# Agent attention with two dense layers on one core: everything up to the sixteenth tile pair written as single-engine steps

## The chip, the cores and the metric

One core of a Trainium2 chip runs the whole program. The metric is the device time of one execution in microseconds (us). Five engines work side by side, each through its own queue in order: TensorE (PE) multiplies matrices, VectorE (DVE), ScalarE (ACT) and GpSimd (POOL) work on elements, and SyncE (SP) issues the transfers. They wait for each other only through semaphores.

## The reference

```python
s = scale * (agents @ k.T); a2k = softmax(s)        # 49 agents over 12480 keys
agent_v = a2k @ v                                   # 49 x 128
x = softmax(scale * (q @ agents.T)) @ agent_v       # 12480 x 128
h = x @ moe_w_in                                    # 128 -> 2048
x = where(h > 0, h, exp(min(h, 0)) - 1) @ moe_w_out # 2048 -> 128
h = x @ moe2_w_in
out = (max(h, 0) + alpha * min(h, 0)) @ moe2_w_out
```

All inputs are float32 except the four weight matrices, which arrive as 64-bit words (float64) and are turned into float32 on the chip.

## The kernel before

The first stretch is the agents' attention over k and v. Both come in ten pieces of 1280 rows (the last of 960, cut into eight chunks of 120). `S0` to `S9` are the score matmuls of a piece: each chunk of 128 keys is the stationary operand and meets `agd`, the agents written twice (98 columns, line 491); the scores go to two PSUM banks and are copied to the tile `S` (501), while VectorE keeps the running maximum `top` (504). The pieces form two halves of five, each with its own maximum: `D` turns the column maxima with a matmul (513), 514 and 515 reduce and spread them, `X` brings them back across (519). `E` subtracts the maximum (524), takes exp (528) and adds up (531, 533). `A` multiplies with v (562). `N` computes the shares of the two halves (543 to 553). Then `normalize` (592 to 594) makes `avn`, the agents' values, and `fold` (603 to 614) multiplies them into the first layer's weights, four slices `s1`, so that layer one becomes one matmul on the query probabilities.

Queries go through in 25 blocks (384, six of 480, eighteen of 512). Their softmax is the chain `q_split` to `q_place`: scores, a 32 by 32 transpose, maximum, exp, sums, weighing, transpose back, and five small transfers that place the result (276, 277).

The layers run in 200 tile pairs u, eight a block, each two chunks of 128 hidden columns. `g1` makes h (630, 633), `g1_act` and `g1_elu` the ELU (640, 641, 648 or 652 and 654), `g2` the product with the second matrix (676, or three matmuls through `mm3`, 431 to 433, once weights and activations are split in a high and a low part), `g3` and `g4` the second layer. `slot(s)` issues two pairs of layer one together with pairs ten behind of layer two.

There are sixteen weight slices w0 to w15, four each of the four matrices. `decode` turns a slice from 64-bit words into float32: two ScalarE reads (`da` 339, `dr` 340), two VectorE bit operations (352, 355), an addition on GpSimd (361, 366), and for the second layer a scaling (370), a rounded copy (372) and a rest (373). `linear` multiplies the alpha part of layer two into one 128 by 128 matrix (390 to 405).

What sets the order: loads follow the table `LOADS`, from a ring of nine buffers for k and v and four for weights. The first stretch follows `ORDER`, in which `T2` advances the decoding and `Q2` the first query chain. In the first stretch and in slots 0 to 10 only SyncE's queue keeps the written order; the other engines' queues are filled by the scheduler from its own estimate of when things are ready. `normalize` and the first two folds between them, and everything from slot 12 on, keep the written order on all queues.

Of the kernel before, what the change touches and what calls it, by code (L numbers as in the profile page):

```python
# [8 lines left out]
F32 = mybir.dt.float32  # L9
# [14 lines left out]
PIECES = [(i * 1280, 10, 128) for i in range(9)] + [(11520, 8, 120)]  # L24
# [33 lines left out]
def agent_attention_moe_kernel(  # L58
# [33 lines left out]
    hps = ctx.enter_context(tc.tile_pool(name="hps", bufs=3, space=bass.MemoryType.PSUM))  # L92
# [20 lines left out]
    agd = const.tile([P, 2, A], F32, name="agd")  # L113
# [69 lines left out]
    def q_max(b):  # L183
        n = blocks[b][1]
        st = q_st[b]
        j = n // 32
        m, m2 = qsmall("m"), qsmall("m2")
        nc.vector.tensor_reduce(out=m[:, :j], in_=by32(st, n), axis=AX.X, op=ALU.max)
        (nc.scalar.copy if b < Q_FIRST else nc.vector.tensor_copy)(out=m2[:32, :j], in_=m[32:, :j])
        q_st[b] = st, m, m2  # L190

    def q_less(b):
        n = blocks[b][1]
        st, m, m2 = q_st[b]
# [47 lines left out]
    def q_norm_4(b):  # L242
# [3 lines left out]
        nc.vector.reciprocal(out=r[:32, :j], in_=s2[:32, :j])  # L246
        (nc.scalar.copy if b < Q_FIRST else nc.vector.tensor_copy)(out=r[32:, :j], in_=r[:32, :j])
        q_st[b] = e, r

    def q_weigh(b):  # L250
# [4 lines left out]
        nc.gpsimd.tensor_tensor(  # L255
# [16 lines left out]
    def q_place(b):  # L272
# [8 lines left out]
        -3: [q_split], 3: [q_scores], 4: [q_sum, q_add], 6: [q_turn], 8: [q_max], 9: [q_less], 11: [q_exp],  # L281
        12: [q_norm_1], 14: [q_norm_2], 15: [q_norm_3], 16: [q_norm_4], 17: [q_weigh], 18: [q_turn], 19: [q_hi],
# [7 lines left out]
    free = {"kv": KV, "w": RAW}  # L290
# [3 lines left out]
    def pump():  # L294
        while todo:
# [7 lines left out]
            if kind == "k":  # L303
                t0, nch, m = PIECES[i]
                kt[i] = rings["kv"].tile([P, 10, P], F32, tag="kv", name="kt").rearrange("p c d -> p (c d)")
                cut = [0, 512, nch * m] if i == 0 else [0, nch * m]
                for lo, hi in zip(cut, cut[1:]):
                    nc.sync.dma_start(out=kt[i][:, lo:hi], in_=kT[:, t0 + lo:t0 + hi])
            elif kind == "v":
                t0, nch, m = PIECES[i]  # L310
                vt[i] = rings["kv"].tile([P, 10, P], F32, tag="kv", name="vt")
                src = vm[:, i * 1280:(i + 1) * 1280] if m == P else vl
                nc.sync.dma_start(out=vt[i][:m, :nch, :].rearrange("p c d -> p (c d)"), in_=src)
# [16 lines left out]
    ahead = []  # L330
    flying = []
    started = [0]

    def decode(i):
        name, j = SLICES[i]
        src = words.pop(i)
        x = dec.tile([P, 4, P], F32, tag="da", name="da")
        r = dec.tile([P, 4, P], U32, tag="dr", name="dr")
        nc.scalar.activation(out=x, in_=src[:, :, :, 1].bitcast(F32), func=AF.Copy, scale=2.0 ** -112)
        nc.scalar.activation(out=r, in_=src[:, :, :, 0], func=AF.Copy, scale=2.0 ** -29)  # L340
        free["w"] += 1
        pump()
        yield
        sl = slice(4 * j, 4 * j + 4)
        if name == "wo1":
            w = wo1w[j] = wo.tile([P, 4, P], F32, tag="wo1", bufs=9, name="wo1w")
            g = w.bitcast(U32)
        else:
            g = w1[j].bitcast(U32) if name in ("wi1", "wo2") else dec.tile([P, 4, P], U32, tag="dg", bufs=2, name="dg")
        t = spare().rearrange("p (f c) -> p f c", c=P).bitcast(U32)  # L350
        xu = x.bitcast(U32)
        nc.vector.tensor_scalar(
            out=t, in0=xu, scalar1=4, scalar2=1, op0=ALU.logical_shift_left, op1=ALU.logical_shift_right
        )
        nc.vector.scalar_tensor_tensor(
            out=g, in0=xu, scalar=0x80000000, in1=t, op0=ALU.bitwise_and, op1=ALU.bitwise_or
        )
        if name in ("wi1", "wo1"):
            done.add(i)
            yield  # L360
            nc.gpsimd.tensor_tensor(out=g, in0=g, in1=r, op=ALU.add)
            return
        h, l = {"wi2": (wi2h, wi2l), "wo2": (wo2h, wo2l)}[name]
        h, l = h[:, sl, :], l[:, sl, :]
        gf = g.bitcast(F32)
        nc.gpsimd.tensor_tensor(out=g, in0=g, in1=r, op=ALU.add)
        yield
        if name == "wo2":
            v = dec.tile([P, 4, P], U32, tag="dg", bufs=2, name="dx").bitcast(F32)
            nc.vector.tensor_tensor(out=v, in0=gf, in1=oma[:, sl].unsqueeze(2).to_broadcast([P, 4, P]), op=ALU.mult)  # L370
            gf = v
        nc.scalar.copy(out=h, in_=gf)
        (nc.vector if i in REST_DVE else nc.gpsimd).tensor_tensor(out=l, in0=gf, in1=h.bitcast(F32), op=ALU.subtract)
        done.add(i)

    def split(j):
        w = wo1w.pop(j)
        h = wo1h[j] = wo.tile([P, 4, P], F32R, tag="wo1", bufs=9, name="wo1h")
# [4 lines left out]
    def linear():

        for j in range(4):
            sl = slice(4 * j, 4 * j + 4)
            t4 = hpair()[:, 0, :].rearrange("p (f c) -> p f c", c=P)
            for f in range(4):
                for x in (wi2h, wi2l):
                    nc.tensor.matmul(t4[:, f, :], x[:, 4 * j + f, :], unit, start=x is wi2h, stop=x is wi2l)  # L390
            kt_ = dec.tile([P, 4, P], F32, tag="da", name="da")
            nc.vector.tensor_tensor(
                out=kt_, in0=t4, in1=al[:, sl].unsqueeze(2).to_broadcast([P, 4, P]), op=ALU.mult
            )
            yield
            tw = hpair()[:, 0, :P]
            for f in range(4):
                nc.tensor.matmul(tw, kt_[:, f, :], w1[j][:, f, :], start=f == 0, stop=f == 3)
            if j == 0:
                nc.vector.tensor_copy(out=lin, in_=tw)  # L400
            else:
                nc.vector.tensor_tensor(out=lin, in0=lin, in1=tw, op=ALU.add)
            yield
        nc.scalar.copy(out=linh, in_=lin)
        nc.vector.tensor_tensor(out=linl, in0=lin, in1=linh.bitcast(F32), op=ALU.subtract)
        done.add("lin")

    lines = linear()
    folded = set()

    def spare():

        return hpair()[:, 0, :] if 0 in o_ps or 0 in y_t or not ahead else bank("o", 1)

    def micro(n):

        while n > 0:
            ran = False
            for x in list(flying):
                if next(x, "end") == "end":  # L420
                    flying.remove(x)
                ran = True
                n -= 1
            if len(flying) < 2 and started[0] in words and (SLICES[started[0]][0] != "wo2" or len(folded) == 4):
                flying.append(decode(started[0]))
                started[0] += 1
            elif not ran:
                return
# [422 lines left out]
```

## Time and profile before

| | |
|---|---|
| three runs, median (lowest to highest) | 1082.84 us (1082.27 to 1084.37) |
| the profiled execution | 1083.18 us |
| its span in the trace | 1081.40 us |
| busy: PE, DVE, ACT, POOL | 97%, 77%, 75%, 57% of the span |

Outside the span lie 1.78 us, of which the trace shows nothing. A busy PE may still be slow: its clock is granted at 1.2 or 2.4 GHz, and its short matmuls are not all at the rate of the array. Shares over the whole span hide that the first tenth looks different from the rest, so the views below cut it in stages.

### The profile page before, as it was taken

To read this page: it belongs to the slowest core of one execution; us is meant where nothing else is said; L and a number is where in the kernel's file an instruction comes from. 1 tells how busy PE (TensorE), PEld (TensorE's weight loads), DVE (VectorE), ACT (ScalarE), POOL (GpSimd) and SP (SyncE) were. 2 spreads that over 40 slices of the span, in tenths; PEclk is the share of its full clock that TensorE was granted. 3 is DMA by queue.
4 is the path that set the end of the run, shared out by engine and by line. 5 is a ranking of instruction groups with operands and counts; after the bars stand their busy time and mean duration, and the time that the engine had idled before them with its cause. 6 is when DMAs were issued, how large, how long until landed. Compare 5 with 4: busy or idle time off the path is not lost.

```text
span 1081.4 us, 13413 instructions
## 1 busy us (share of the span) xinstructions
PE 1053.1 (97%) x5029; PEld 831.9 (77%) x5029; DVE 830.9 (77%) x932; ACT 811.1 (75%) x944; POOL 613.4 (57%) x349
## 2 busy tenths in 40 slices
PE   7788999999999999999999999999999999999998
PEld 6635888888888777777777777777777777777776
DVE  5866687878878788788788788788787787787653
ACT  5587677777777877877877877777777777777763
POOL 3656655665555665565565565565565566555440
PEclk9888999999999999999999999999999999999999
DMA  9920000000010010010010010000000000000000
GB/s 357 375 89 19 20 8 28 19 19 20 20 29 10 20 30 10 20 30 10 21 30 10 21 30 13 26 22 15 25 20 19 22 20 20 20 10 20 11 1 20
DMA packets 17915, 41.34 MB, mean 38 GB/s; under 512 B 3345, under 2 KB 6303, under 8 KB 17851
## 3 DMA queue, kind: packets, MB, share of 16 engines
q1 hardware_dynamic: 17707, 40.36, 11.5%
q8 instruction: 40, 0.66, 0.3%
q14 instruction: 24, 0.20, 0.1%
q10 hardware_dynamic: 144, 0.13, 0.0%
HBM read 27.60 MB, written 6.39 MB: 31 GB/s over the span
## 4 chain that ended last, share of the span: by engine, by line
PE 91%; DVE 3%; ACT 2%; DMA 2%; issue 1%; POOL 1%; SPq 0%; DVEq 0%; POOLq 0%; ACTq 0%
PE o L431 10%; PE o L433 9%; PE o L432 9%; PE h L630 8%; PE h L433 8%; PE h L431 8%; PE h L432 8%; PE y L431 8%; PE y L432 8%; PE y L433 8%; PE h L633 4%; DMA kt<-in_kT_dram 1%; DMA wi<-in_w_in_dram 1%; PE h L159 1%; ACT e L640 0%
## 5 line engine op out<-in xcount | busy, mean ns | idle before, releaser
L665 POOL TENSOR_TENSOR gl<-g,gh 128x1024 fp32r<-128x1024 f32 (+1 forms) x192 | 454.0, 2370 | 258.4 <-DVE gh L654 170.7
L706 DVE SCALAR_TENSOR_TENSOR xl<-h,xh 128x1024 fp32r<-128x1024 f32 (+3 forms) x201 | 239.7, 1192 | 127.4 <-ACT xh L705 125.8
L705 ACT ACTIVATE xh<-h 128x1024 fp32r<-128x1024 f32 (+3 forms) x201 | 201.3, 1002 | 177.3 <-PE h L433 175.9
L652 DVE SCALAR_TENSOR_TENSOR g<-e,h 128x1024 f32<-128x1024 f32 (+1 forms) x192 | 229.0, 1193 | 71.6 <-ACT e L641 55.5
L640 ACT ACTIVATE e<-h 128x1024 f32<-128x1024 f32 (+2 forms) x200 | 199.2, 996 | 30.2 <-PE h L633 26.4
L641 ACT ACTIVATE e<-e 128x1024 f32<-128x1024 f32 (+2 forms) x200 | 207.9, 1040 | 6.1
L431 PE MATMUL o<-xh,wo2h 128*128 128x512 f32 (+2 forms) x400 | 162.1, 405 | 2.8 <-ACT xh L705 2.8
L433 PE MATMUL o<-xh,wo2l 128*128 128x512 f32 (+2 forms) x400 | 154.5, 386 | 0.0
L433 PE MATMUL h<-yh,wi2l 128*128 128x512 f32 (+2 forms) x400 | 154.4, 386 | 0.0
L431 PE MATMUL h<-yh,wi2h 128*128 128x512 f32 (+2 forms) x400 | 154.4, 386 | 0.0
L432 PE MATMUL o<-xl,wo2h 128*128 128x512 f32 (+2 forms) x400 | 154.3, 386 | 0.0
L432 PE MATMUL h<-yl,wi2h 128*128 128x512 f32 (+2 forms) x400 | 154.1, 385 | 0.0
L431 PE MATMUL y<-gh,wo1h 128*128 128x512 f32 (+1 forms) x384 | 149.1, 388 | 0.0
L432 PE MATMUL y<-gl,wo1h 128*128 128x512 f32 (+1 forms) x384 | 148.4, 386 | 0.0
L433 PE MATMUL y<-gh,wo1l 128*128 128x512 f32 (+1 forms) x384 | 148.3, 386 | 0.0
L654 DVE SCALAR_TENSOR_TENSOR gh<-e,h 128x1024 fp32r<-128x1024 f32 (+1 forms) x96 | 115.0, 1198 | 0.0
L630 PE MATMUL h<-pst,s 128*128 128x512 f32 (+2 forms) x400 | 110.6, 396 | 3.2 <-DVE gh L648 1.0
L431 PEld LDWEIGHTS o<-xh,wo2h 128*128 128x128 f32 x400 | 75.1, 188 | 32.1 <-ACT xh L705 14.7
L663 ACT CAST gh<-g 128x1024 fp32r<-128x1024 f32 (+1 forms) x96 | 98.7, 1028 | 1.1 <-DVE g L652 1.1
L630 PEld LDWEIGHTS h<-pst,s 128*128 128x128 f32 x400 | 75.0, 190 | 22.3 <-issue 1.9
L431 PEld LDWEIGHTS h<-yh,wi2h 128*128 128x128 f32 x400 | 75.4, 188 | 14.7 <-issue 0.2
L433 PEld LDWEIGHTS o<-xh,wo2l 128*128 128x128 f32 x400 | 75.3, 188 | 14.6
(149 smaller groups left out, 1302.9 us busy)
## 6 DMA issues: line engine op xcount, KB each, us to landing
vt<-in_vm_dram SPq DMA_DIRECT2D x9, 640.0 KB
kt<-in_kT_dram SPq DMA_DIRECT2D x8, 640.0 KB
q<-in_qT_dram SPq DMA_DIRECT2D x18, 256.0 KB
psq<-pst SPq DMA_DIRECT2D x72, 64.0 KB
out_dram<-o SPq DMA_DIRECT2D x17, 256.0 KB
wi<-in_w_in_dram SPq DMA_DIRECT2D x8, 512.0 KB
wo<-in_w_out_dram SPq DMA_DIRECT2D x8, 512.0 KB
q<-in_qT_dram SPq DMA_DIRECT2D x6, 240.0 KB
```

What stands on the lines that cost most here:

```text
L431: nc.tensor.matmul(out, w_hi, x_hi, start=start, stop=False)
L432: nc.tensor.matmul(out, w_hi, x_lo, start=False, stop=False)
L433: nc.tensor.matmul(out, w_lo, x_hi, start=False, stop=stop)
L630: nc.tensor.matmul(h_t[u + v][:, c, :], s1[:, i + 2 * v + c, :], pst[b][:, :n], start=True, stop=False)
L640: nc.scalar.activation(out=e, in_=h_t[u], func=AF.Relu, scale=-1.0)
L641: nc.scalar.activation(out=e, in_=e, func=AF.Exp, scale=-1.0)
L652: nc.vector.scalar_tensor_tensor(out=g, in0=e, scalar=-1.0, in1=h, op0=ALU.add, op1=ALU.max)
L654: nc.vector.scalar_tensor_tensor(out=gh, in0=e, scalar=-1.0, in1=h, op0=ALU.add, op1=ALU.max)
L663: nc.scalar.copy(out=gh, in_=g)
L665: nc.gpsimd.tensor_tensor(out=gl, in0=g, in1=gh.bitcast(F32), op=ALU.subtract)
L705: nc.scalar.activation(out=xh[:, c, :], in_=h[:, c, :], func=AF.Relu)
L706: nc.vector.scalar_tensor_tensor(out=xl[:, c, :], in0=h[:, c, :], scalar=0.0, in1=xh[:, c, :].bitcast(F32), op0=ALU.max, op1=ALU.subtract)
```

## The change

`ORDER` becomes a list of about 530 steps, one for one engine each, from the first score matmul to the last step ahead of slot 16; every engine's queue keeps that order from the start, and `slot` begins at 16. Decoding falls into eight steps (`x r t o a v h l`), the ELU of a pair into `e`, `E`, `g.`, `gc`, `gl`, the query chain into its single instructions. A list `OTHER` puts some of them on another engine than usual. The piece of k and v at the end is cut into 128-row chunks and one of 64 rows. A score chunk becomes two matmuls of 64 keys by 49 agents in two column halves, and a piece's scores fit one PSUM bank, six of which go round. The maxima `mc` and the shares are kept in PSUM, and the shares are applied to the values instead of to the turning matrix. `LOADS` brings k and v ahead of most weights.

```diff
 LOADS = """
-    w0 k0 w1 k1 q0 w2 k2 w3 k3 w4 k4 k5 w5 k6 k7 k8 k9 w6 v0 v1 w7 v2 v3 v4 w8 v5 v6 w9 v7 v8 w10 v9 a0 q1
-    w11 w12 w13 w14 w15
+    k0 q0 k1 k2 k3 k4 k5 k6 k7 w0 z0 w1 k8 k9 v0 v1 v2 v3 v4 v5 q1 v6 w2 v7 v8 w3 v9 w4 w5 w6 w7 w8 w9 w10 a0 w11
+    w12 q2 q3 w13 w14 w15
 """
 ORDER = """
-    T2 S0 T2 S1 Q2 T2 S2 Q2 S3 T2 Q2 S4 D0 Q2 T2 S5 X0 E0 Q2 S6 T2 E1 Q2 S7 E2 T2 S8 Q2 E3 T2 Q2 S9 D1 E4 A0 X1 A1 T2
...
+    S0 q0.qh q0.ql C0 q0.sc S1 q0.sl q0.sa q0.t1 S2 C1 M1 q0.mx S3 M2 C2 q0.m2 q0.ms q0.mc M3 S4 C3 q0.d q0.ex C4 S5
...
+OTHER = """
+    C0 C4 C5 K1 K7 e11 e13 e15 e2 e6 e8 l9 q0.wg v11 v13 v15 v9
+""".split()
+FIRST = 16
...
         def scores(i):
-            sp = hpair()
-            for c in range(nch):
-                o = sp[:m, c // 5, 2 * A * (c % 5):2 * A * (c % 5) + 2 * A]
-                nc.tensor.matmul(o, kt[i][:, c * m:(c + 1) * m], ag, start=True, stop=True)
+            sp[i] = single()[:, :10 * A].rearrange("p (c a) -> p c a", a=A)
+            for c in range(nch):
+                for p0 in (0, AP):
+                    col = c * m + p0 * (PIECES[i][0] + c * m + p0 < NTOK)
+                    nc.tensor.matmul(sp[i][p0:p0 + AP, c, :], kt[i][:, col:col + AP], ag, start=True, stop=True)
...
-            nc.vector.tensor_tensor(out=mc[:, 2:3], in0=mc[:, 0:1], in1=mc[:, 1:2], op=ALU.max)
-            nc.vector.tensor_scalar(out=cs, in0=mc[:, 0:2], scalar1=mc[:, 2:3], scalar2=None, op0=ALU.subtract)
+        mc = across[:, AP + 4:AP + 6]
+                nc.vector.tensor_reduce(out=rs[:, 4:5], in_=mc, axis=AX.X, op=ALU.max)
+                nc.vector.tensor_tensor(out=cs, in0=mc, in1=rs[:, 4:5].to_broadcast([P, 2]), op=ALU.subtract)
...
+    def negative(u):
+        e = e_t[u] = wide("e", F32, of(u)[2])
+        if f"e{u}" in OTHER:
+            nc.vector.tensor_scalar(out=e, in0=h_t[u], scalar1=0.0, scalar2=None, op0=ALU.min)
+        else:
+            nc.scalar.activation(out=e, in_=h_t[u], func=AF.Relu, scale=-1.0)
```

The first place is SyncE's queue at the start. Its rows before (`kt` is a piece of k, `wi` and `wo` a weight slice, `agp` the agents):

```order
L440 DMA agp<-in_agT_dram 128x64
L317 DMA wi_149<-in_w_in_dram 128x1024
L308 DMA kt<-in_kT_dram 128x512
L308 DMA kt<-in_kT_dram 128x768
L317 DMA wi_154<-in_w_in_dram 128x1024
L308 DMA kt<-in_kT_dram 128x1280
```

and now:

```order
L510 DMA agp<-in_agT_dram 128x64
L348 DMA kt<-in_kT_dram 128x512
L348 DMA kt<-in_kT_dram 128x768
L150 DMA q<-in_qT_dram 128x384
L348 DMA kt<-in_kT_dram 128x1280 x7
L358 DMA wi_168<-in_w_in_dram 128x1024
```

The first weight slice moved from ahead of the first piece of k to behind the eighth; further on, eleven weight slices stood ahead of the last piece of v, and four do now.

The second place is VectorE from the second maximum on. Before (`pm<-top` and `su<-acc` close a half's maximum and sum, `h<-da` and the row with `da,h` decode):

```order
L506 TENSOR_REDUCE pm<-top 128x49
L352 TENSOR_SCALAR h<-da 128x512
L514 TENSOR_REDUCE mc<-o 128x1
L524 TENSOR_TENSOR S<-S,o 128x490
L355 SCALAR_TENSOR_TENSOR wo1w<-da,h 128x512
L515 COPY mb<-mc 49x128
L543 TENSOR_TENSOR mc<-mc 128x1
L544 TENSOR_SCALAR cs<-mc 128x2
L524 TENSOR_TENSOR S<-S,o 128x490 x4
```

and now, where `o` is the PSUM bank that holds the maxima:

```order
L579 TENSOR_REDUCE pm<-top 128x49
L405 SCALAR_TENSOR_TENSOR w_1_95<-da,hb 128x512
L592 TENSOR_REDUCE o<-o 128x1
L593 COPY mb<-o 49x128
L665 TENSOR_REDUCE rs<-o 128x1
L666 TENSOR_TENSOR cs<-o,rs 128x2
L603 TENSOR_TENSOR S<-S,o 128x490 x2
L603 TENSOR_TENSOR S<-S,o 128x392
L603 TENSOR_TENSOR S<-S,o 128x490 x2
```

The small steps read PSUM instead of the tile `mc`, and one decoding row stands here instead of two.

The third place is VectorE behind the last row of the first stretch, the copy to `avn` (`s` and `s1q` are a fold's results, `gh` the ELU of a pair). Before:

```order
L593 COPY avn<-o 128x128
L352 TENSOR_SCALAR o<-da 128x512
L355 SCALAR_TENSOR_TENSOR w_0_97<-da,o 128x512
L352 TENSOR_SCALAR o<-da 128x512
L611 SCALAR_TENSOR_TENSOR s_84<-hi,low,h 128x512
L614 TENSOR_TENSOR s1q<-h,hi 128x128
```

and now:

```order
L685 COPY avn<-o 128x128
L391 TENSOR_SCALAR o<-da 128x512
L405 SCALAR_TENSOR_TENSOR wo1w<-da,o 128x512
L391 TENSOR_SCALAR o<-da 128x512
L405 SCALAR_TENSOR_TENSOR wo1w<-da,o 128x512
L716 SCALAR_TENSOR_TENSOR s_81<-hi,low,h 128x512
L719 TENSOR_TENSOR s1q<-h,hi 128x128
```

Two slices are decoded between the copy and the first fold's result, and they are the first ones of `moe_w_out` (`wo1w`), which before were decoded ahead of the copy.

## Rows read from the trace of the kernel before

**Rows 1.** The page: granted TensorE clock in 40 slices, tenths of full speed.

```profile
PEclk9888999999999999999999999999999999999999
```

**Rows 2.** Stages: length, busy us (count) by engine, clock, DMA share, GB/s.

```profile
0.00:59.13 59.13, 42.58 (x419) 39.18 (x419) 37.93 (x72) 33.25 (x68) 30.59 (x43) 0.94 0.95 348
59.13:103.30 44.17, 36.35 (x133) 18.07 (x134) 32.00 (x51) 35.67 (x62) 25.87 (x24) 0.84 0.14 47
103.30:143.78 40.48, 40.23 (x228) 35.11 (x227) 29.02 (x41) 27.11 (x34) 24.76 (x14) 0.96 0.05 13
143.78:1081.40 937.62, 933.94 (x4254) 739.51 (x4252) 731.97 (x769) 715.08 (x783) 532.22 (x269) 1.00 0.07 19
```

**Rows 3.** TensorE in order of time: start, us, line, operands, count [idle before].

```profile
13.71 2.44 PE L491 MATMUL h<-agd,kt 128*128 128x98 f32 x20
...
24.27 0.44 PE L513 MATMUL o<-ident,pm 128*64 128x128 f32 x4 [0.17 <-DVE pm L506]
...
30.59 4.12 PE L491 MATMUL h<-agd,kt 128*128 128x98 f32 x36 [0.72 <-ACT S L501]
34.64 2.39 PE L562 MATMUL y<-vt,S 128*49 128x128 f32 x40
...
58.20 0.54 PE L592 MATMUL o<-by,avs 128*128 128x160 f32 x2 [0.69 <-DVE avs L571]
59.13 1.12 PE L603 MATMUL h<-w,avn 128*128 128x512 f32 x2 [0.39 <-DVE avn L593]
...
72.26 2.93 PE L676 MATMUL y<-gh,wo1w 128*128 128x384 f32 x4
```

**Rows 4.** Stages of the loading, columns as in rows 2.

```profile
0.00:20.00 20.00, 12.74 (x87) 12.24 (x88) 9.07 (x22) 11.76 (x25) 7.74 (x22) 1.00 0.90 339
20.00:40.00 20.00, 17.68 (x183) 16.45 (x182) 17.67 (x31) 12.85 (x25) 13.24 (x14) 1.00 1.02 410
40.00:50.00 10.00, 5.48 (x68) 5.08 (x70) 7.87 (x12) 4.49 (x10) 6.35 (x7) 0.75 1.03 374
```

**Rows 5.** SyncE, then ScalarE, in order of time.

```profile
40.08 0.41 SPq L313 DMA_DIRECT2D vt<-in_vl_dram  x1
...
5.55 0.66 ACT L339 ACTIVATE da<-wi 128x512 f32<-128x512 f32 x1 [2.23 <-DMA wi<-in_w_in_dram]
```

**Rows 6.** VectorE, groups by form: count, busy us, mean ns, idle before.

```profile
L352 DVE TENSOR_SCALAR h<-da 128x512 uint32<-128x512 uint32 x11 | 7.5, 686 | 5.0 <-ACT da L339 4.8
L648 DVE SCALAR_TENSOR_TENSOR gh<-e,h 128x768 f32<-128x768 f32 x8 | 7.5, 936 | 5.3 <-ACT e L641 5.2
L506 DVE TENSOR_REDUCE pm<-top 128x49 f32<-128x490 f32 x2 | 2.0, 1011 | 0.1
```

**Rows 7.** VectorE in order of time, around the second maximum.

```profile
39.19 1.01 DVE L515 COPY mb<-mc 49x128 f32<-49x128 f32 x1
40.13 1.23 DVE L543 TENSOR_TENSOR mc<-mc 128x1 f32<-128x1 f32 x1
41.40 1.16 DVE L544 TENSOR_SCALAR cs<-mc 128x2 f32<-128x2 f32 x1
42.47 2.85 DVE L524 TENSOR_TENSOR S<-S,o 128x490 f32<-128x490 f32 x5
...
53.54 0.16 DVE L546 TENSOR_TENSOR rs<-o,cs 128x2 f32<-128x2 f32 x1 [0.38 <-PE o L542]
```

**Rows 8.** GpSimd in order of time, the same stretch.

```profile
40.07 1.27 POOL L361 TENSOR_TENSOR wo1w<-wo1w,dr 128x512 uint32<-128x512 uint32 x1
41.30 1.23 POOL L531 TENSOR_TENSOR acc<-S,acc 128x490 f32<-128x490 f32 x1
```

**Rows 9.** ScalarE and GpSimd, groups by form.

```profile
L340 ACT ACTIVATE dr<-wo 128x512 uint32<-128x512 uint32 x8 | 5.4, 670 | 0.3 <-POOL wo1w L361 0.3
L366 POOL TENSOR_TENSOR dg<-dg,dr 128x512 uint32<-128x512 uint32 x4 | 5.1, 1277 | 4.3 <-DVE dg L355 4.2
```

**Rows 10.** ScalarE in order of time: one weight slice handed over.

```profile
49.74 0.62 ACT L372 CAST wi2h<-dg 128x512 fp32r<-128x512 f32 x1 [2.50 <-POOL dg L366]
```

More of the change, by code (lines that the diff above doesn't have):

```diff
@@ L383, in linear @@
[L383 to L403, printed above, removed]
+            wo1w[j] = wo.tile([P, 4, P], F32, tag="wo1", bufs=9, name="wo1w")
@@ L404, in linear, with lin_high, lin_low @@
+    def lin_high(_):
         nc.scalar.copy(out=linh, in_=lin)
+    def lin_low(_):
         nc.vector.tensor_tensor(out=linl, in0=lin, in1=linh.bitcast(F32), op=ALU.subtract)
         done.add("lin")
[L408 to L428, printed above, removed]
@@ L555, in values, with total, total_down @@
+        @step("Z")
+        def total(h):
+            nc.vector.tensor_reduce(
+                out=su[:, h, :A], in_=acc[:, h].rearrange("p c a -> p a c"), axis=AX.X, op=ALU.add
+            )
+        @step("W")
+        def total_down(h):
+            for t in range(2):
+                nc.tensor.matmul(den[AP * t:AP * t + AP, h:h + 1], su[:, h, :], ones, start=True, stop=True)
+        @step("A")
         def values(i):
@@ L584, in prologue, with even, odd @@
-        assert not stages and all(i in done for i in range(4)), (stages, done, started)
-        return across
-    def normalize(across):
+        @step("Ba")
+        def even(h):
+            nc.scalar.activation(
+                out=avs[:A, h, :], in_=av["y"][:A, 256 * h:256 * h + P], func=AF.Copy, scale=cs[:A, h:h + 1]
+            )
+        @step("Bd")
+        def odd(h):
+            nc.vector.tensor_scalar(
+                out=avs[AP:AP + A, h, :], in0=av["y"][AP:AP + A, 256 * h:256 * h + P],
+                scalar1=cs[AP:AP + A, h:h + 1], scalar2=None, op0=ALU.mult,
+            )
@@ new lines, in run_step @@
+    def run_step(x):
+        if x[0] == "q" and "." in x:
+            Q_ONE[x[3:]](int(x[1]))
+            return
+        name = x.rstrip("0123456789")
+        arg = x[len(name):]
+        if x[0] == "B":
+            name, arg = "B" + x[2], x[1]
+        STEPS[name](int(arg) if arg else 0)
+    work = None
+    with ExitStack() as early:
+        steps = ORDER.split()
+        with tc.manual_schedule():
+            att = early.enter_context(tc.tile_pool(name="att", bufs=1))
+            rings["kv"] = early.enter_context(tc.tile_pool(name="kv", bufs=KV))
+            pools["hb"] = early.enter_context(tc.tile_pool(name="hb", bufs=6, space=bass.MemoryType.PSUM))
+            prologue(att)
+            while steps[0] != "f0":
+                run_step(steps.pop(0))
@@ L795, in slot @@
         ask(3)
-        if s == LINES + 2:
-            next(lines, None)
-        if 2 <= s <= 8:
-            split(s // 2 - 1)
-    with tc.manual_schedule(engines=PINNED):
-        for s in range(0, AUTO, 2):
-            slot(s)
-            if s == 0:
-                fold(2)
-                fold(3)
     with tc.manual_schedule():
-        for s in range(AUTO, U + L2 + 2, 2):
+        for x in steps:
+            run_step(x)
+        for s in range(FIRST, U + L2 + 2, 2):
             slot(s)
```

479 lines of the change are left out of this document (303 added, 176 removed).

## Prediction

> **What bounds the kernel now.** I read the page's row of granted clock first: the clock is short of full only in slices 2 to 4 of 40, some 27 to 108 us [rows 1]. The stages come next [rows 2]. From 143.78 us to the end TensorE is busy 933.94 of 937.62 us at clock 1.00, and the same slots stand there in both kernels, so nothing can move in it but its start. The change lives ahead of 143.78, where slot 18 starts its first matmul; by then both kernels have done the same TensorE work. I cut there at the first fold, 59.13 us [rows 3].
>
> Stretch one, up to 59.13: TensorE is busy 42.58 us, so it idles 16.6. Stretch two, 59.13 to 143.78, lasts 84.65: busy 36.35 + 40.23 = 76.6, idle 8.1. Its clock is 0.84 and 0.96; with the low level half the high one, that is 2 x (0.16 x 44.17 + 0.04 x 40.48) = 17.4 us at 1.2 GHz, so up to 8.7 us of the busy time is slowness. What could be won at all is therefore 16.6 + 8.1 + 8.7 = 33 us less what any order leaves.
>
> In stretch one the DMA is busy 0.95 of the time [rows 2] and brings 339, 410 and 374 GB/s [rows 4]: 6.8 MB by 20 us, 15.0 by 40, 18.7 by 50. The last piece of v is issued at 40.08 [rows 5], behind eleven weight slices of 0.52 MB, 12.8 MB of k and v and 0.2 MB of the first query block, 18.8 MB: it is there at some 50. Its matmuls come ahead of the turn at 58.20 and the fold at 59.13 [rows 3]. So the loading bounds stretch one at first, and the attention's chain of small VectorE steps behind it.
>
> **The change part by part.** *Loads.* Four weight slices instead of eleven stand ahead of the last piece of v, which is then the 15.3rd MB and arrives at some 41 us. The first half-piece of k, 0.26 MB, takes the place of the first weight slice, 0.52 MB, which ScalarE had at 5.55 [rows 5]. I start S0 at 4.5 us.
>
> *Scores.* A piece takes 2.44 us for 20 issued matmuls, 0.122 each: two passes for each of ten chunks of 98 columns [rows 3]. Now it takes 40, half as wide in both operands. The nearest row is the v product, also in alternating column halves: 40 in 2.39 us, 0.060 each, with 128 columns [rows 3]. I take 2.4 us a piece, no change. Bounds: 40 x 0.122 = 4.9 us, if half the width saves nothing, and 1.2, if all scales.
>
> The Trainium skill ("TensorEngine Tiling (Array Packing)", Instruction Overhead) speaks against this edit: each matmul carries about 60 cycles of overhead, and a factor should not be taken from a dimension that is already small. By it the 20 added matmuls of a piece would cost up to 20 x 25 ns = 0.5 us, 5 us in all if nothing hides them; the row of 0.060 us for a matmul that would stream 128 columns twice as long alone says that the halves overlap.
>
> *VectorE from the first maximum to the fold.* X0 stands behind S7. Eight pieces are 19.5 us; two query matmuls and D0 and X0 I take at 0.44 each, like the D row [rows 3], 1.8 together: 4.5 + 19.5 + 1.8 = 25.8 us. By then 5.5 MB are needed and 6.8 are there at 20, so the DMA is no longer what ends last. From X0 to the turn VectorE's new queue holds 39 rows. 26 are full-width: five of 490 columns in succession take 2.85, 0.57 each, and a bit operation 0.686 [rows 6, 7]; at 0.62 that is 16.1. Three are reductions of 1.01 [rows 6], 3.0. Ten are small; 0.16 is the cheapest [rows 7], at 0.22 that is 2.2. Half a microsecond waits for X1 behind a v product. Sum 21.8, so the turn starts at 47.6, and from there to the fold is 59.13 - 58.20 = 0.93 [rows 3]: 48.5. **Stretch one gains 10.6 us.** Bounds: 45 us with every full-width row at 0.57 and S0 at 3.5; 54 if the three rows here that VectorE now does with both operands in SBUF each stand behind a GpSimd row of 1.28 [rows 9], 3.8, and the small steps below wait for 2.
>
> *Small steps in PSUM.* This is inside that sum: the copy to `mb` and the two steps on `mc` take 1.01, 1.23 and 1.16 us for next to no data, and the last two end at 41.36 and 42.56 where GpSimd's rows end, at 41.34 and 42.53 [rows 7, 8], while a like step on PSUM takes 0.16 [rows 7]. I take 0.2 to 0.3 for each of the new ones, a gain of 2.5; if they wait all the same, they cost those 2.5 again.
>
> The Trainium skill ("SBUF — State Buffer", Who interferes with whom) says that a VectorE instruction with two SBUF inputs, or in a two-port mode, waits until a GpSimd instruction that reads SBUF has ended, and that one with a single SBUF input does not. By that rule the trace agrees, with the two ends within 0.03 us. It speaks for the steps in PSUM and against the rows of `OTHER` that bring two SBUF operands to VectorE (K1, K7, l9, q0.wg): by it up to 5 us more, spread over both stretches.
>
> *What goes into stretch two.* Less is decoded ahead of the fold. Counted in the two orders, 9 slices had their bit operations on VectorE by then and 4 have now; of ScalarE's reads 11 pairs and 5; of GpSimd's additions 9 and 4. VectorE gets 5 x 2 x 0.65 = 6.5, six ELU minima at about 1.0 (0.936 is the nearest of that size [rows 6]) and loses four scalings and five query rows of about 0.65: +6.5 + 6.0 - 5.5 = +7. ScalarE gets 6 x 2 x 0.6 of the 0.67 that a read shows [rows 9], three rounded copies more, and loses the six: +4. GpSimd gets five additions, two rests, four scalings and one more rest at 1.28 [rows 9]: +15. Busy in stretch two before: VectorE 61.0, ScalarE 62.8, GpSimd 50.6 [rows 2]. After: 68, 67, 66.
>
> *What that costs.* None of the three exceeds the 84.65 that the stretch lasts, and TensorE needs 76.6 - 8.7 = 68 at full clock, so four engines want 66 to 68 each. From the fold to the first y matmul is 13.1 us [rows 3]; its ten steps are of the sizes above, 0.3 to 1.1 us, 7 in all, and the new queues put some 3 us of decoding between them: 10, a gain of 3. Against it, VectorE had 23.6 us idle and keeps 16.6; I let a third of its 7 us show, 2.5. One query block's scores move into stretch one, 0.7. Net -1.2. **Stretch two: 83.4.** Bounds: 72, the fullest engine's 68 and 4 us ahead of its start; 94, if VectorE is no busier than before (61.0 / 84.65 = 72%, 68 / 0.72).
>
> *Sum.* 48.5 + 83.4 = 131.9 against 143.78, 11.9 less. Against the profiled execution's 1083.18 us (span 1081.40 and 1.78 outside) that is 1071.3; that execution lies 0.34 above the median shown, so **1071**.
>
> **The rivals.** *Packed tighter.* The written order fills four queues at once and stretch two nears 75: 1083 - 10.6 - 9.7 = 1062. For it: only 8.1 us of the old stretch two is TensorE idling and 8.7 is low clock, both from gaps of the kind that a better order closes. Against: 68 of 75 us on every engine leaves a tenth for all hand-overs.
>
> *The gain is given back.* VectorE stays at 72%, the stretch takes 94, and 10.6 - 9.7 leaves nothing: 1082. For it: the idle time there is mostly waits on another engine's row, like the 2.50 us in which ScalarE waited for a slice's addition [rows 10]; more work makes no such wait shorter.
>
> *Slower: slices queue up behind each other.* A slice now crosses ScalarE, VectorE, GpSimd, ScalarE and GpSimd or VectorE again, in queues that a late row blocks for the ELU rows behind it. Eleven slices are left at the fold. If each exposes on VectorE one wait of 3 us, near the 2.50 of [rows 10], that is 33 on top of 68: 101, 16 over the old stretch, less 10.6: 1089. It decides from 84.65 + 10.6 - 68 = 27 us of idle VectorE; before it idled 23.6. Against: the waits lie beside each other as long as two slices are under way.
>
> *Slower: half-width scores cost as much as whole ones.* At 4.9 a piece X0 comes 20 us later and the whole attention tail behind S9; the fold lands near 66 and the end near 1089. It decides from 3.6 us a piece. The v product's 0.060 speaks against.
>
> *Low clock.* The early layer matmuls come sparser if TensorE starts sooner and waits more; rows show 17.4 us at 1.2 GHz in stretch two [rows 2]. Ten more would cost up to 5: inside the forecast's range.
>
> **How the numbers follow.** The forecast (8 to 16 us less) 0.48, its own range 1067 to 1075. Tighter 0.18. A smaller gain, 2.2 to 8 us, 0.11. Given back 0.08. Slower by slices 0.11, by scores 0.04. About 2.2 us, 0.2%, is what a measurement can tell from none. Faster 0.48 + 0.18 + 0.11 = 0.77, same 0.08, slower 0.15. For 8 in 10 the range reaches from 1060 (stretch one at 45, two at 75) to 1083 (given back).
>
> **What would show it.** In the new trace: S0 at 4 to 5 us and 2.2 to 2.6 us between score pieces; the first fold at 45 to 52; the steps on `mc` at 0.3 or below; the first y matmul some 10 us behind the fold; VectorE at 78 to 85% between the fold and slot 18, whose first matmul starts at 128 to 136. From there to the end 937 us as before. The forecast is wrong if the fold comes after 54, if slot 18 starts ahead of 126 or behind 140, or if the last stage is not 936 to 939 long.

## The result, and the profile after

The changed kernel takes **1066.03 us** (median of 4 runs, 1065.06 to 1066.79); the kernel before, beside it on the same chip, 1083.61 (1082.27 to 1085.41). Ratio 0.9836, 95% interval 0.9818 to 0.9854: 17.6 us less, where 11.9 were forecast and 8 to 16 was the forecast's own range. The profiled execution is the one of 1065.06 us, span 1063.1.

The stages after, cut at the first fold and at slot 18 as in [rows 2], and between them at the first matmul of the second dense layer (H0; the 103.30 of [rows 2] is another event): length, busy us (count) by engine, granted clock, DMA share, GB/s.

```profile
0.00:47.27 47.27, 33.84 (x616) 29.18 (x617) 32.34 (x69) 22.31 (x49) 17.47 (x34) 1.00 0.96 366
47.27:87.72 40.45, 32.65 (x154) 17.91 (x155) 37.15 (x58) 37.28 (x65) 33.40 (x29) 0.91 0.42 134
87.72:125.84 38.12, 38.12 (x202) 33.74 (x203) 33.49 (x44) 27.52 (x38) 31.45 (x23) 0.96 0.06 14
125.84:1063.10 937.26, 933.83 (x4254) 739.53 (x4252) 731.77 (x769) 715.17 (x782) 532.48 (x269) 1.00 0.07 19
```

The last stage is as before, 937.26 against 937.62 us. Stretch one ends at 47.27 instead of 59.13, 11.9 us earlier. Stretch two lasts 40.45 + 38.12 = 78.57 instead of 84.65, 6.1 less. From 87.72 to slot 18 TensorE is never idle; up to there VectorE and ScalarE are busy 92% each and TensorE 81%.

TensorE after, in order of time, answering to [rows 3] (start, us, line, operands, count, idle before and what ended it):

```profile
4.12 1.10 PE L562 MATMUL hb<-ag,kt 128*64 128x49 f32 x16 [4.12 <-DMA kt<-in_kT_dram]
...
9.72 10.02 PE L562 MATMUL hb<-ag,kt 128*64 128x49 f32 x240 [0.31 <-DMA kt<-in_kT_dram]
...
20.86 1.32 PE L562 MATMUL hb<-ag,kt 128*64 128x49 f32 x40
22.46 0.42 PE L598 MATMUL o<-ident,mb 49*128 49x49 f32 x2 [0.28 <-DVE mb L593]
...
43.23 1.07 PE L640 MATMUL y<-vt,S 128*49 128x128 f32 x14 [0.84 <-DMA vt<-in_vm_dram]
...
47.27 1.12 PE L697 MATMUL h<-w,avn 128*128 128x512 f32 x2 [0.38 <-DVE avn L685]
...
51.18 0.97 PE L734 MATMUL h<-pst,s 128*128 128x384 f32 x4 [1.02 <-DVE s L716]
52.08 0.45 PE L737 MATMUL h<-psq,s1q 32*128 32x384 f32 x4
...
56.69 2.90 PE L803 MATMUL y<-gh,wo1w 128*128 128x384 f32 x4
```

Forty half-width matmuls take 1.32 us, 0.033 each; twenty whole ones took 2.44. The releasers before the pieces of k and v are now mostly transfers. The chain of the first 60 us, followed back from its end, says the same of the part ahead of the fold (start, us, what):

```profile
21.03 11.56 DMA vt<-in_vm_dram
...
32.66 10.53 DMA vt<-in_vm_dram
...
43.23 1.44 PE y L640 x16
...
44.75 0.37 ACT avs L651
...
45.15 0.37 DVE avs L657
...
45.54 0.37 ACT avs L651
...
45.94 0.37 DVE avs L657
```

The last piece of v lands at 43.2, and four short rows wait for each other behind its product. VectorE had to wait for the first of them:

```profile
45.15 0.36 DVE L657 TENSOR_SCALAR avs<-y,cs 49x128 f32<-49x128 f32 x1 [1.03 <-ACT avs L651]
```

VectorE around the second maximum, answering to [rows 7]:

```profile
32.45 0.28 DVE L593 COPY mb<-o 49x128 f32<-49x128 f32 x1
32.66 0.14 DVE L665 TENSOR_REDUCE rs<-o 128x1 f32<-128x2 f32 x1
32.83 0.16 DVE L666 TENSOR_TENSOR cs<-o,rs 128x2 f32<-128x2 f32 x1
```

The copy and the two steps take 0.28, 0.14 and 0.16 us where they took 1.01, 1.23 and 1.16.

### The profile page after: what moved, and what is told of

Same layout as the page of the kernel before. It is cut to its first block, busy times and chain, and to the rows that moved or that the text cites. A ratio compares the mean times of both kernels' runs of the same rounds, so it can differ in the third digit from the quotient of the medians.

```text
span 1063.1 us, 13811 instructions
## 1 busy us (share of the span) xinstructions
PE 1038.4 (98%) x5225; PEld 820.4 (77%) x5225; DVE 834.8 (79%) x938; ACT 802.3 (75%) x932; POOL 614.8 (58%) x352
## 4 chain that ended last, share of the span: by engine, by line
PE 92%; DMA 3%; DVE 2%; ACT 1%; POOL 1%; issue 1%; SPq 0%; POOLq 0%; ACTq 0%; DVEq 0%
PE o L486 11%; PE o L488 9%; PE o L487 9%; PE h L486 8%; PE h L488 8%; PE h L487 8%; PE h L734 8%; PE y L486 8%; PE y L488 8%; PE y L487 8%; PE h L737 4%; DMA vt<-in_vm_dram 2%; PE hb L562 1%; DMA kt<-in_kT_dram 1%; PE h L183 0%
## 5 line engine op out<-in xcount | busy, mean ns | idle before, releaser
L848 DVE SCALAR_TENSOR_TENSOR xl<-h,xh 128x1024 fp32r<-128x1024 f32 (+2 forms) x195 | 234.0, 1200 | 122.0 <-ACT xh L847 120.5
L847 ACT ACTIVATE xh<-h 128x1024 fp32r<-128x1024 f32 (+2 forms) x195 | 196.6, 1008 | 171.7 <-PE h L488 170.4
L744 ACT ACTIVATE e<-h 128x1024 f32<-128x1024 f32 (+1 forms) x184 | 185.3, 1007 | 26.8 <-PE h L737 24.6
L745 ACT ACTIVATE e<-e 128x1024 f32<-128x1024 f32 (+1 forms) x184 | 193.2, 1050 | 5.8
L173 POOL TENSOR_TENSOR ql<-q,qh 128x512 fp32r<-128x512 f32 (+2 forms) x25 | 31.7, 1267 | 95.9 <-ACT qh L168 91.8
```

Of the source, the lines that this page charges most:

```text
L744: nc.scalar.activation(out=e, in_=h_t[u], func=AF.Relu, scale=-1.0)
L745: nc.scalar.activation(out=e, in_=e, func=AF.Exp, scale=-1.0)
L847: nc.scalar.activation(out=xh[:, c, :], in_=h[:, c, :], func=AF.Relu)
L848: nc.vector.scalar_tensor_tensor(out=xl[:, c, :], in0=h[:, c, :], scalar=0.0, in1=xh[:, c, :].bitcast(F32), op0=ALU.max, op1=ALU.subtract)
```

## The experiments

The theory from these rows: in stretch one loading ends last, and the gain there is the new order of loads together with a written order that can follow it. In stretch two the engines' added work fills waits that were there before. The rivals give the gain to the half-width scores, to the steps in PSUM, to VectorE's balance, or to the clock. Each ratio is to the kernel before on the same chip in the same session: e1 to e4 stood together, e5 to e8, and e9 to e12. So a run of the first two groups is compared with the control e9 by its ratio.

| run | median us | ratio to before, 95% |
|---|---|---|
| after, unchanged (e9) | 1067.09 | 0.9844 (0.9831 to 0.9858) |
| before, new loads alone (e1) | 1106.16 | 1.0205 (1.0190 to 1.0221) |
| two idle loads (e2) | 1069.69 | 0.9866 (0.9852 to 0.9879) |
| whole chunks, 49 columns (e3) | 1087.23 | 1.0028 (1.0019 to 1.0037) |
| small steps in SBUF (e4) | 1067.10 | 0.9845 (0.9831 to 0.9858) |
| whole chunks, 98 columns (e5) | 1069.33 | 0.9871 (0.9852 to 0.9891) |
| minima on ScalarE (e6) | 1069.51 | 0.9864 (0.9851 to 0.9878) |
| pairs on GpSimd (e7) | 1067.49 | 0.9842 (0.9827 to 0.9857) |
| filling matmuls (e8) | 1071.10 | 0.9886 (0.9866 to 0.9906) |
| sums in two tiles (e10) | 1066.73 | 0.9839 (0.9825 to 0.9852) |
| changed place of the order (e11) | 1068.12 | 0.9853 (0.9840 to 0.9867) |
| all three (e12) | 1068.23 | 0.9867 (0.9849 to 0.9886) |

**The control first**, since it says what a difference is worth.

> The kernel after, unchanged, beside the other three on the same chip: 1064.5 to 1067.5, and from its trace how far the first fold wanders with the loads (47.3 so far; 46 to 49).

TensorE, the last v product and the first fold:

```profile
43.95 1.07 PE L640 MATMUL y<-vt,S 128*49 128x128 f32 x14 [0.97 <-DMA vt<-in_vm_dram]
...
48.34 2.08 PE L697 MATMUL h<-w,avn 128*128 128x512 f32 x2 [0.38 <-DVE avn L685]
```

The same program: v lands 0.7 us later, the fold at 48.34, and the fold's two matmuls take 2.08 instead of 1.12 because the clock had already fallen to 1.2 GHz (granted 0.50 from 47 to 53 us). The clock of its stretch two is 0.90 against 0.93. So differences of about 1 us between profiles, and of 0.0015 between ratios, are not read as effects below.

**Loads alone, in the kernel before.**

```
-    w0 k0 w1 k1 q0 w2 k2 w3 k3 w4 k4 k5 w5 k6 k7 k8 k9 w6 v0 ... w10 v9 a0 q1
+    k0 q0 k1 k2 k3 k4 k5 k6 k7 w0 w1 k8 k9 v0 v1 v2 v3 v4 v5 q1 v6 w2 v7 v8 w3 v9 w4 ... a0
```

> The kernel before, with its table of loads alone replaced: k and v first, four weight slices ahead of the last piece of v as in the kernel after. Nothing else is changed. Theory (the loads are what the written order lives on): the last piece of v lands near 42 us instead of 51, but the old steps find no slice to decode between the score pieces, so decoding moves behind: first fold at 51 to 54, stretch two longer by most of that, total 1076 to 1084. Rival (loads alone are the gain of stretch one): first fold at 47 to 49 and the total 1071 to 1073, some 11 us less, with stretch two as before.

It is 22 us slower than before. ScalarE in order of time:

```profile
19.68 0.66 ACT L339 ACTIVATE da<-wi 128x512 f32<-128x512 f32 x1 [12.34 <-DMA wi<-in_w_in_dram]
```

It stands 12.34 us at a weight slice. TensorE meanwhile:

```profile
3.96 4.50 PE L491 MATMUL h<-agd,kt 128*128 128x98 f32 x20 [3.96 <-DMA kt<-in_kT_dram]
21.84 4.59 PE L491 MATMUL h<-agd,kt 128*128 128x98 f32 x20 [13.38 <-DVE w L355]
```

The old order still puts the first slice's reads ahead of the first score copy. That slice now comes behind eight pieces of k, and TensorE waits 13.38 us for a buffer that the slice's VectorE row holds. Both stated outcomes are wrong; the theory had the direction (loads need the order), not the size. In the kernel before, the new load order alone costs time; it needs steps in a matching order. The reverse, the new order of steps with the old loads, was not tried, so the two shares of the gain are not told apart.

**Two idle loads ahead of v.**

```
-    ... k8 k9 v0 v1 v2 v3 v4 ...
+    ... k8 k9 v0 d0 v1 v2 d1 v3 v4 ...
+            elif kind == "d":
+                nc.sync.dma_start(out=rings["idle"][:, i, :], in_=w_in["wi2"][:, :512].bitcast(U32))
```

> The kernel after, with two more loads of 0.52 MB each, read by nobody, ahead of the last pieces of v. Theory (loading bounds stretch one): 1.05 MB at the 0.37 to 0.39 MB/us of this stretch is 2.7 us; the last piece of v, the first fold and the end come 2.5 to 2.9 us later, 1068.6 to 1069.0. Rival (VectorE's chain bounds it, as the prediction summed it): v lands later, but fold and end by less than 0.7 us, since VectorE was done only 1 us ahead of them.

The same two rows of TensorE:

```profile
45.39 1.07 PE L642 MATMUL y<-vt,S 128*49 128x128 f32 x14 [0.90 <-DMA vt<-in_vm_dram]
...
49.74 2.07 PE L699 MATMUL h<-w,avn 128*128 128x512 f32 x2 [0.38 <-DVE avn L687]
```

The last product comes 2.2 us later than in the trace of after and 1.4 later than in the control's, the fold 2.5 and 1.4. The end is 2.6 us behind the control's median, 0.0022 in the ratio: a little above the stated 1068.6 to 1069.0, and far from the rival's 0.7. So a megabyte ahead of v shows in the fold, by half to nearly all of the 2.7 us, depending on the trace that it is held against. Seven slices fewer stand ahead of v in the change, 3.7 MB; at the 410 GB/s of [rows 4] that is, by estimate, some 9 of the 11.9 us of stretch one.

**The small steps back in SBUF.**

```
-        mc = across[:, AP + 4:AP + 6]
+        mc = att.tile([P, 2], F32, name="mc")
```

> The kernel after, with the two maxima's tile of two columns back in SBUF, so that the copy and the two steps on it read SBUF. Theory (v's landing bounds the fold, these steps have slack ahead of it): they take 0.5 to 1.2 us each again, where GpSimd runs beside them, and the total moves by less than 0.6. Rival (the prediction's 2.5 us): first fold 1.5 to 2.5 later, total 1067.5 to 1068.5.

VectorE in order of time:

```profile
32.76 1.07 DVE L666 TENSOR_TENSOR cs<-mc,rs 128x2 f32<-128x2 f32 x1
```

And GpSimd beside it:

```profile
32.54 1.27 POOL L413 TENSOR_TENSOR w<-w,dr 128x512 uint32<-128x512 uint32 x1
```

The step on two columns takes 1.07 us again and ends at 33.83, where GpSimd's row ends at 33.81. The wait lies inside the row's own time, with no idle time ahead of it; so semaphores are not the only way in which these engines hold each other up. The Trainium skill ("SBUF — State Buffer", Who interferes with whom) has VectorE wait in this way beside a GpSimd row that reads SBUF, when both VectorE's operands lie in SBUF; the trace agrees, and the step with one input, on `mc` alone, kept its 0.14. The copy took 0.43 instead of 0.28. So the edit brought back 1.1 us of the 2.5 that the prediction booked, and the total is the control's: these 1.1 us are hidden behind v's landing. Whether all 2.5 would be is not shown; VectorE's wait for the sums, 1.03 us in the trace of after, leaves room for about 1.

**Whole chunks instead of halves**, with 49 columns and then with 98.

```
             for c in range(nch):
+                if PIECES[i][0] + c * m + P <= NTOK:
+                    nc.tensor.matmul(sp[i][:, c, :], kt[i][:, c * m:c * m + P], ag, start=True, stop=True)
+                    continue
```

```
+                    n = min(2 * A, 512 - c * A)
+                    nc.tensor.matmul(wide_[:, c * A:c * A + n], kt[i][:, c * m:c * m + P], agd[:, :n], ...)
```

> The kernel after, with each chunk's scores as one matmul of 128 columns again (10 a piece instead of 20; the output is the same). Theory (a piece waits for its load, so its matmuls' time is hidden): a piece takes longer than the 1.25 us of two halves, up to 2.5, but the first fold moves by less than 0.6 us and the total by less than 1. Rival (the halves are a third of the gain of stretch one): eight pieces at 1.2 us more ahead of X0, fold 3 us later or more, total 1069 or above.

> The kernel after, with each chunk's scores as one matmul of 128 rows against the doubled agents, 98 columns, as in the kernel before (the second 49 are overwritten by the next chunk). It tells apart why the 49-column chunks cost 21 us. Theory (49 columns behind a full load of 128 leave TensorE too idle for its clock to rise; 98 do not): after a slow start as in the kernel before a piece takes 2.4 to 2.5 us, the two passes 0.12 each; X0 at 27 to 28, first fold at 50 to 52, total 1069 to 1071. Rival (whole chunks are slow by themselves in this order): 4.5 us a piece again, total 1085 or more.

With 49 columns, TensorE in order of time:

```profile
34.93 0.70 PE L590 MATMUL o<-ident,pm 128*64 128x128 f32 x4
35.56 4.50 PE L561 MATMUL hb<-ag,kt 128*128 128x49 f32 x20
39.99 0.66 PE L601 MATMUL o<-ident,mb 49*128 49x49 f32 x2
```

The weight loads of its score matmuls, grouped (count: min/median/max ns):

```profile
L561 PEld LDWEIGHTS hb<-ag,kt x105: 333/333/333, 11.7 to 33.9; 128*128 128x128 f32 x105
```

With 98 columns, TensorE in order of time:

```profile
9.97 13.62 PE L565 MATMUL hb<-agd,kt 128*128 128x98 f32 x120 [0.89 <-DMA kt<-in_kT_dram]
...
23.89 2.45 PE L565 MATMUL hb<-agd,kt 128*128 128x98 f32 x20
26.27 0.42 PE L605 MATMUL o<-ident,mb 49*128 49x49 f32 x2
...
49.52 2.07 PE L704 MATMUL h<-w,avn 128*128 128x512 f32 x2 [0.39 <-DVE avn L692]
```

And its weight loads:

```profile
L565 PEld LDWEIGHTS hb<-agd,kt x122: 186/192/192, 10.0 to 24.0; 128*128 128x128 f32 x122
```

Half the columns make a piece nearly twice as long, 4.50 against 2.45 us. It is not the matmul alone: the same weight load takes 333 instead of 192 ns, and the untouched rows of `pm` and `mb` 0.70 and 0.66, where [rows 3] have 0.44 and the trace of after 0.42. By their size these are durations of 1.2 GHz, like the fold's 2.08 instead of 1.12 us at a granted 0.50 in the control; they were kept up for some 45 us in which TensorE was never idle, until the v products came. The row of the granted clock does not show it (last section). Theory e5 holds in the pieces and in the total; X0 at 26.27 and the fold at 49.52 came 0.7 and 0.5 us ahead of its ranges. The theory for e3 that the loads would hide this falls, and the rival's number (1069 or above) was passed for another reason than its 1.2 us a piece. Against the control the halves are worth 2.2 us here (0.0027 in the ratio); doubling the agents to 98 columns was what kept the old form out of these slow 45 us.

**Balance of the engines.**

```
-    C0 C4 C5 K1 K7 e11 e13 e15 e2 e6 e8 l9 q0.wg v11 v13 v15 v9
+    C0 C4 C5 K1 K7 l9 q0.wg v11 v13 v15 v9            (e6)
+    C0 C4 C5 e11 e13 e15 e2 e6 e8 v11 v13 v15 v9      (e7)
```

> The kernel after, with the six ELU minima of VectorE (tiles 2, 6, 8, 11, 13, 15) back on ScalarE. VectorE has 6 us less in stretch two, ScalarE 6 to 7 more. Theory (VectorE, busy 90% there, is not what bounds it: its added work fell into its own waits, and ScalarE's chain of minimum, exponential and reads is as long): no gain, 1066 to 1069. Rival (VectorE bounds stretch two): 3 us or more less, 1063 or below.

> The kernel after, with the four rows of two SBUF operands that it gives to VectorE (two sums of the attention, one rounding rest, one query weighting) back on GpSimd. Theory (they hold up VectorE by little: 0.90 and 0.67 us for the two sums, against 1.28 for a GpSimd row of this size): GpSimd gains 5 us of work, fold and end later by 0.5 to 2 us, 1066.5 to 1068. Rival (VectorE's wait for the SBUF port costs more than the row is worth): the end up to 2 us earlier, 1064 to 1065.

The stage of e6 from the fold to H0:

```profile
48.65:91.07 42.42, 34.11 (x154) 18.05 (x155) 34.87 (x55) 38.97 (x67) 33.00 (x29) 0.86 0.37 122
```

VectorE falls from 37.15 to 34.87 us, ScalarE rises to 38.97, and the stage grows by 2.0; the end is 2.4 later than the control's (0.0020 in the ratio), half a microsecond above the theory's range. So relief of VectorE, busy 92%, gained nothing. That ScalarE's share of the same chain is as long is read from the busy times and not tested apart; the clock, 0.86 against 0.91, is in the 2.0 us too. e7 can't be told from the control, in its stated range; the four rows of two SBUF operands cost nothing that shows at the end.

**Clock and order in stretch two.**

```
-    ... x7 G0 ...  e1 t7 f2 ...  t13 G10 ...  q2.mx H0
+    ... x7 zz8 G0 ...  e1 t7 zz12 f2 ...  t13 zz5 G10 ...  q2.mx zz6 H0     # and 11 between G10's halves
+            nc.tensor.matmul(idle_t[0][:, 384:], unit, unit, start=True, stop=True)     # zz: so many
```

> The kernel after, with matmuls of no use (a unit matrix by itself, into 128 columns of PSUM that nothing reads) in five places where TensorE waits between the first fold and 88 us: 8, 12, 5, 11 and 6 of them at 0.11 us, about as long as each wait. Theory (the two spells at 1.2 GHz, 53.7 to 60.3 and 87.6 to 91.0 us, follow from these waits): the granted clock stays 1.00 in both, the later one gives back 1.7 us, the earlier up to 1 more since VectorE sets the pace there: 1063.3 to 1064.5. Rival (the clock falls all the same, or what it gives back is waited for elsewhere): 1065.5 to 1067.

Two stages behind the fold, which began at 48.55 here (the cuts are those of the trace of after):

```profile
47.27:57.00 9.73, 8.84 (x61) 4.88 (x60) 9.19 (x18) 9.25 (x19) 6.44 (x7) 1.00 0.71 229
57.00:82.00 25.00, 20.82 (x105) 13.09 (x106) 22.95 (x35) 23.80 (x43) 21.58 (x18) 1.00 0.42 136
```

TensorE stands at the first of the late ones:

```profile
86.18 1.33 PE L891 MATMUL y<-unit 128*128 128x128 f32 x5 [2.82 <-ACT yh L788]
```

With the early filling the clock stayed at 1.00 up to 82 us in this trace, but the first y product still came 9.4 us behind the fold, as in after, and the last one of block 0 was only 0.8 us nearer to it (23.9 behind the first, not 24.8): TensorE's clock did not set the pace there. The late filling waited 2.82 us for ScalarE's read of the tile that it wrote into, and the clock fell there (0.69 from 82 to 92 us). So the end, 1071.10, is 4 us behind the control and worse than both stated outcomes; that is this edit's fault, and the later spell stays untested by it.

```
-    q2.sa a12 Y6 q3.qh t15 e9 e8 l11 h12 nc1 o15 E9 l12 Y7 q2.t1 E8 g.9 ... yh x14 t13 G10 yl o13 gl8 nd1 ...
+    q2.sa a12 Y6 t15 e9 e8 l11 nc1 o15 E9 Y7 E8 g.9 nd1 gc9 yh g.8 h12 q3.qh gl9 l12 ... G10 yl q2.t1 t13 o13 gl8 ...
```

> The kernel after, with one place of the fixed order changed: between G8 and H0 (79 to 88 us) the ELU rows of tiles 8 and 9, their rounding and the rounding of y stand ahead of a rounded slice, a query split, a query transpose and a bit operation on ScalarE and VectorE. TensorE's own order is the same. Theory (from 79 to 88 us the chain minimum, exponential, ELU sets the pace, and TensorE's waits of 0.74, 1.43 and 0.81 us there bring on the spell at 1.2 GHz): G10's second half 1 us earlier, H0 1 us earlier, end 0.8 to 2.5 us earlier than the control. Rival (the rows put off are late for something behind H0): the end within 0.4 of the control or later.

TensorE in order of time, H0 and the wait behind it:

```profile
86.38 0.41 PE L486 MATMUL h<-yh,wi2h 128*128 128x384 f32 x1 [0.86 <-ACT qh L168]
90.73 0.77 PE L487 MATMUL y<-gl,wo1h 128*128 128x480 f32 x1 [2.61 <-POOL gl L777]
```

H0 came 27.9 us behind the first y product instead of 31.0 (30.5 in the control), more than the theory had. Then TensorE waited 2.61 us for GpSimd's rounding rest (`gl`), which the same edit had pushed behind a slice's; the end, 1.0 us behind the control's, is the rival's.

```
-                out=avs[:A, h, :], in_=av["y"][:A, ...]          # ScalarE: one half of each sum; VectorE: the other
+            for p in (slice(0, A), slice(AP, AP + A)):          # ScalarE: both halves of h = 0; VectorE: of h = 1
+                ... out=avs[h][p, :], in_=av["y"][p, ...]
```

> The kernel after, with the two halves of the scaled sums in two tiles, one written by ScalarE alone and one by VectorE alone, instead of one tile written by both in turn. In the trace of after these four rows of 0.36 us wait for each other from 44.75 to 46.30. Theory (stretch one ends with v's landing and this chain): two lie beside each other, from the end of the v product to the first fold 0.7 to 0.9 us less, and the same at the end. Rival (VectorE is full behind the fold, the gain is given back there): fold earlier, end within 0.4 of the control.

> The two edits together (sums in two tiles, the changed place of the order), and the 8 and 12 matmuls of no use in the first two waits of TensorE behind the fold, which kept the clock at 1.00 there and brought the y product at 82 us 0.8 us nearer to the fold. Theory: 0.8 + 1.2 + 0.7 us, 1062.5 to 1064 where the control has 1066. Rival (each only moves a wait): within 0.5 of the better of the two alone.

Two tiles end within 0.4 us of the control, but the edit didn't do what it was for: in the profile of e10, its longest execution (1069.05), v landed at 45.0 and the fold came at 50.38, not earlier. VectorE in e12, where v landed as in after:

```profile
45.80 0.71 DVE L660 TENSOR_SCALAR avs<-y,cs 49x128 f32<-49x128 f32 x2 [1.45 <-ACT avs L653]
```

Its two rows still stand until ScalarE's two are done, and from the last v product to the fold it is 4.2 us as in after (4.0). Both engines read one PSUM tile; whether that is why they wait is not shown. What the chain would give if it were split stays open. The fold of e12 came at 47.69 at 1.2 GHz, and so did the filling behind it; the second line is the stage from the fold to the first y product:

```profile
56.77 2.82 PE L892 MATMUL y<-unit 128*128 128x128 f32 x12
...
47.69:61.92 14.23, 14.23 (x58) 7.81 (x58) 10.70 (x19) 10.36 (x20) 7.43 (x9) 0.50 0.39 138
```

It takes 0.24 us each instead of the 0.13 of e8 and outlasts the waits that it was to fill. TensorE was busy for all 14.23 us of this stage, and the granted clock was 0.50 throughout. e12 ends at 1068.23, outside both stated outcomes. No version beat the changed kernel by more than the control wanders.

## Why the forecast held, and where it did not

The gain was forecast too small: 1066.03 us lies below the forecast's own range of 1067 to 1075, the control's 1067.09 at its edge, and both inside the wider one of 1060 to 1083. Slot 18 came 6.1 us earlier than forecast in the trace: 1.2 of them fall in stretch one, 4.8 in stretch two.

**Stretch one, 48.5 forecast, 47.27 and 48.34 measured.** S0 at 4.12 and the small steps came as said, but what ended last did not. The prediction summed VectorE's queue from X0 to the turn and held that the DMA no longer ends last. In the traces v's landing ends last (43.2, forecast 41), VectorE has waited 1.03 us for the sums by then, and e2 moves the fold with the bytes, while e4 does not move it with 1.1 us more on VectorE. That the wrong path gave the right number is in part luck: X0 came at 22.46 instead of 25.8, which alone would have brought the turn 3.3 us forward, and v landed 2.2 us late. With X0 back at 26.27, in e5, the last product no longer waits for v, and the fold comes at 49.52. The lower bound of 45 does not follow from its terms either: 26 rows at 0.57 take off 1.3 us and S0 at 3.5 another 1.0, which leaves 46.2.

**The score piece, 2.4 us forecast, 1.3 measured: mis-sized.** The row chosen was the v product's 0.060 us with 128 moving columns; 49 columns take 0.033, near the lower bound of 1.2 a piece. e5 puts 2.45 back: X0 at 26.27, as the prediction had it (25.8), and 2.2 us on the end. The overhead that the prediction took from the Trainium skill ("TensorEngine Tiling (Array Packing)", Instruction Overhead), up to 0.5 us more a piece, did not come: the piece became 1.1 us shorter. That a matmul has no fixed cost is not shown by this, since 0.060 scaled by the columns alone would be 0.023.

**Stretch two, 83.4 forecast, 78.57 and 79.51 measured: the term that failed.** The fold to the first y product took 9.4 to 9.9 us (forecast 10). The miss is behind it: "I let a third of its 7 us show" and TensorE's need held constant. VectorE's work rose by 9.6 us, from 61.02 to 70.64, so that it is busy 90% of the stretch (forecast 78 to 85%), and none of it shows as a wait of TensorE: TensorE's idle time there is 7.8 us, and was 8.1. TensorE's own busy time fell from 76.6 to 70.8 us (72.5 in the control, whose clock is lower) for the same work less one query block. One pair of lines, the first-layer matmuls, fell by about as much. Their busy time in stretch two of the kernel before, first the full ones, then those of 32 rows:

```profile
59.13:143.78 84.65, 12.43 (x37) 7.12 (x37) 0.90 0.10 31
...
59.13:143.78 84.65, 7.11 (x36) 2.81 (x36) 0.90 0.10 31
```

And in the control, at the same clock of 0.90:

```profile
48.34:127.85 79.51, 9.90 (x36) 6.30 (x37) 0.90 0.24 73
...
48.34:127.85 79.51, 4.52 (x36) 1.82 (x36) 0.90 0.24 73
```

19.5 us became 14.4 (14.9 in the trace of after). They come in groups of four full ones and four of 32 rows, for two tile pairs. In order of time, one such group in the kernel before:

```profile
78.14 0.80 PE L630 MATMUL h<-pst,s 128*128 128x384 f32 x2
78.88 0.44 PE L633 MATMUL h<-psq,s1q 32*128 32x384 f32 x2
80.30 0.62 PE L630 MATMUL h<-pst,s 128*128 128x384 f32 x2 [0.98 <-DVE gh L648]
80.85 0.44 PE L633 MATMUL h<-psq,s1q 32*128 32x384 f32 x2
```

Both kernels write four and four. The old order had five of the nine groups ahead of slot 18 pulled apart into two and two; the fixed order keeps the 32-row ones together in all nine (0.45 at 52.08). Four 32-row matmuls take 0.45 us, and two take 0.44, so each parted group paid them twice. The Trainium skill ("TensorE: Matmul & The Clock Gate", Measured speedup vs the span model) says that row tiles issued together span little more than one matmul; the trace agrees. 5 x 0.44 = 2.2 us of the 5.1 are this. Parted full ones cost something too, 0.62 us for two (80.30) against 0.97 for four (51.18), by estimate some 0.27 a group; the rest I take to be where the spells at 1.2 GHz fell. All this is read from the traces and not shown by an edit. The parted groups all begin ahead of 103.30, where 7.8 of TensorE's 8.1 us of waiting lie as well, and in e8 a full clock up to 82 us moved the last y product by only 0.8. So what the shorter matmuls are worth at the end, and with it the cause of the larger gain in stretch two, stays open.

**Slot 18** started at 125.84 (127.85 in the control), both ahead of the 128 to 136 that were forecast, and the first a hair ahead of the 126 from which the prediction called itself wrong; 937 us followed as said. Of the rivals "packed tighter" (1062) is the nearest; it named TensorE's gaps and its low clock; the gaps stayed at 7.8 us and the clock at 0.90 to 0.93 (0.90 before), while its busy time got shorter. Slices queueing up did not come; e1 and e11 show what one late row does to those behind it where an order is wrong, 12 and 2.6 us at one row.

## What to carry to other kernels

Change a load order only together with the order of the engines that consume it: one early step on a late load blocks its whole queue. When a scheduler may part row-tiled matmuls, look whether they still stand together before you hold TensorE's time constant. Before moving work to relieve an engine that is busy 90%, ask whether the engine that gets it is in the same chain.

## What was not expected of the hardware

A TensorE that is never idle can stay at 1.2 GHz: in e12 the granted clock was 0.50 for 14.23 us without a gap. In e3, with whole chunks and 49 moving columns, the durations say the same for some 45 us; in e5, with 98 columns, not. The view of the granted clock says 1.00 for these 45 us, as for the first microseconds of every run, where the durations say otherwise (the first 20 score matmuls of e5 took 4.30 us, later ones 2.45). It seems to show 1.00 until a first change is recorded; the durations of known rows are the better witness there.

Half-width fp32 matmuls in alternating column halves follow each other every 0.033 us, against 0.11 to 0.12 for whole ones of twice the moving columns: a piece of the same scores in half the time.
